# Seven-product down projection for all eight pairs of tiles, with h of tiles 0–3 normalised on GpSimd

## The chip, the cores and the metric

The kernel runs on one core of a Trainium2 chip. The metric is device time in microseconds (us) of one execution. The profile covers one execution; its span is about 2 us shorter than the measured time. PE is TensorE, PEld its weight load, DVE is VectorE, ACT is ScalarE, POOL is GpSimd, SP issues the DMA. "L244" is line 244 of the kernel that is being profiled; the change moves most lines by a few, so the table of lines below gives both numbers. In the profile lines `arena` is the kernel's on-chip buffer, `ps` the eight accumulator banks that TensorE writes, and `x8` a count.

## The reference, cut to what matters

```
xn = layernorm(x)                                  # x is 2048 x 512
# A: linear attention, 32 heads of 16, q, k, v = xn @ wqkv
phi = concat(softmax(p), softmax(-p))              # for q and k, p = q @ w_phi or k @ w_phi
kv  = sum over tokens of phi_k^T v;  z = sum of phi_k
A   = (phi_q kv / phi_q z) @ wo
# B: bilinear gated unit, F = 1792
h   = (xn @ w_gate) * (xn @ w_up)
out = x + A + h @ w_down
```

Layernorm of a token is a subtraction of the mean and a factor `rstd`. Everything in B is linear in that factor twice, so h of a token that was not normalised is right up to a factor r2 = rstd². The kernel uses this for its first four tiles (of 128 tokens), in order to start the matmuls before the statistics are there.

## The kernel before

A list scheduler inside the kernel decides in which order each engine gets its instructions; each engine then runs its own list strictly in order and waits on semaphores. TensorE alternates between 56 gate units (8 matmuls of 512 columns; ScalarE copies the gate half, VectorE multiplies it with the up half) and the features of queries and keys.

The features hand work round the engines: TensorE makes p, ScalarE takes two exponentials, VectorE sums, ScalarE inverts, and GpSimd scales the second softmax. The query buffers are a ring of three (`RQ = 3`).

```python
def features(name, t, w, b=None):                  # w = 0: query, 1: key
    s = t % (RK if w else RQ)
    ...                                            # (cut: matmul, two exps on ACT)
    dve(lambda e: e.tensor_reduce(out=sm, in_=e_v, axis=AX.X, op=ALU.add), ...)         # L511
    ...                                            # (cut: 1/sum on ACT)
    pool(lambda e: e.tensor_tensor(out=rat, in0=sm[:, :, 0], in1=rs[:, :, 1], op=ALU.mult), ...)   # L519
    pool(lambda e: e.tensor_tensor(out=e_v[:, :, 1, :], in0=e_v[:, :, 1, :], ...)       # L521
```

The down projection has two forms. Tiles 0–3 use `out_tile`, 18 matmuls of 512 columns each, because r2 can then be applied at the eviction. Tiles 4–15 use `out_pair`: two tiles of h and w_down are cut into 2 x 2 blocks, and seven products replace eight (7 x 7 matmuls, and 16 for the attention heads: 65 of 256 columns). It needs sums and differences of the blocks, in half precision, made by VectorE (`h_combine`, `wd_combine`). These mix two tiles, so r2 must be in h before them.

```python
def out_tile(t, between):                          # tiles 0-3
    mm(ps, [(hT_v[:, ft, tok], wdh_v[:, ft, :]) for ft in range(NF)], ..., stop=False)  # 14 x 512 columns
    between()
    mm(ps, [(oT_tile(t)[:, q, :], wo_v[:, q, :]) for q in range(NQ)], ..., start=False) # 4 x 512 columns
    dve(lambda e: e.scalar_tensor_tensor(out=stg, in0=ps, scalar=ri[:, t:t + 1], in1=xr_tile(t), ...)

def d_scale():                                     # powers of two that keep h and w_down in fp16's range
    power_of_two(swd, ...)
    pool(lambda e: e.tensor_tensor(out=scl[:, 22:23], in0=sh, in1=swd, op=ALU.mult), ["sh", "swd"], ["both"], 1)
    dve(lambda e: e.reciprocal(out=scl[:, 23:24], in_=scl[:, 22:23]), ["both"], ["rboth"], 1)
```

The last two lines matter later: a product of two single numbers sits in GpSimd's list, and VectorE's list holds an instruction that waits for it.

The softmax here doesn't subtract the row's maximum and nothing guards it: scores larger than these inputs give would overflow.

Of the kernel before, what the change touches and what calls it, by code (L numbers as in the profile page):

```python
# [24 lines left out]
ND = 4  # L25
# [28 lines left out]
class _Sched:  # L54
# [10 lines left out]
    def _record(self, st, reads, writes, free=()):  # L65
        deps = {}

        def need(d, raw):
            if d is None or d is st:
                return  # L70
            if d.lane == st.lane and (st.eng == PE or not raw):
                return
            deps[id(d)] = d

        for k in reads:
            assert k in self.writer, f"{k} is read unwritten"
            need(self.writer.get(k), True)
            self.readers.setdefault(k, []).append(st)
        for k in writes:
            w = self.writer.get(k)  # L80
            assert w is None or w is st or self.readers.get(k) or k in reads or st.lane == w.lane or k in free, f"{k} is overwritten unread"
            need(w, False)
            for r in self.readers.get(k, ()):
                need(r, False)
            self.writer[k] = st
            self.readers[k] = []
        st.deps = list(deps.values())
# [36 lines left out]
def _build(nc, es, A_x, A_wqkv, A_w_phi, A_wo, B_w_gate, B_w_up, B_w_down, out):  # L124
# [210 lines left out]
    load_gu(SP, 3)  # L335
    sc.pin = False
# [230 lines left out]
    epsz = sbf("epsz", 0, 1)  # L567
    kvz_v = sb("kvz", 0, 8 * CW).rearrange("p (c j) -> p c j", c=8)

    def kv_finish():  # L570
        sc.prio = 0
        for hb in range(2):
            dve(lambda e, hb=hb: e.tensor_tensor(
                out=kvz_v[:, hb * 4:hb * 4 + 4, :], in0=bank(hb, 0, 4 * CW).rearrange("p (c j) -> p c j", c=4),
                in1=mask[:, None, :].to_broadcast([128, 4, CW]), op=ALU.mult),
                [("ps", hb), "mask"], [("kvz", hb, 0)], 4 * CW)
            z = bank(hb, 0, 4 * CW).rearrange("p (c h j) -> p c h j", c=4, h=4)[:, :, :, 16]
            mz = mask.rearrange("p (h j) -> p h j", h=4)[:, None, :, 16].to_broadcast([128, 4, 4])
            oz = kvz_v[:, hb * 4:hb * 4 + 4, :].rearrange("p c (h j) -> p c h j", h=4)[:, :, :, 16]
            dve(lambda e, z=z, mz=mz, oz=oz: e.scalar_tensor_tensor(out=oz, in0=z, scalar=epsz, in1=mz, op0=ALU.add,  # L580
                                                                    op1=ALU.mult),
                [("ps", hb), "mask", "epsz", ("kvz", hb, 0)], [("kvz", hb)], 16)
        sc.prio = 1
# [25 lines left out]
    def num_stage(t):  # L609
        ph = ph_tile(t)  # L610
        b0 = 2 * (t % 2) if t < ND else 0
# [13 lines left out]
        k, key = upscale(t)  # L625
        act(den_v[:, r], nd[:, :, :, 16], ps, [("den", r)], func=ACTF.Ln)
        act(w_v[:, r], den_v[:, r], [("den", r), key], [("w", r)], func=ACTF.Exp, scale=-1.0, bias=k)
# [15 lines left out]
    ri, lnup = scl[:, 4:4 + ND], scl[:, 26:26 + ND + 1]  # L643

    def upscale(t):
        return (lnup[:, t + 1:t + 2] if t < ND else lnup[:, 0:1]), "lnup"

# [3 lines left out]
    def squares(src, i, after):  # L651
        j = NF - 8 + squared[0] % 8
        squared[0] += 1
        junk = hT_v[:, j, 3 * 512:4 * 512]
        if src == "wd":
            i_ap, key, col, o_ap = wd_v[:, i, :], ["wd"], 28 + i, junk
        else:
            v, col = (wg_v, i) if src == "wg" else (wu_v, 14 + i)
            i_ap, o_ap = v[:, :, i * 128:(i + 1) * 128], junk.rearrange("p (a b) -> p a b", a=NQ)
            key = [(src, max(k for k, (lo, _) in enumerate(SLICES) if lo <= i * 128))]  # L660
        act(o_ap, i_ap, key + after + ([("junk", j)] if squared[0] > 8 else []), [("junk", j), ("ssq", col)],
            func=ACTF.Square, accum=ssq[:, col:col + 1])
# [20 lines left out]
    def h_scale():  # L683
        norms(0, 28, 2)
        pool(lambda e: e.tensor_tensor(out=scl[:, 20:21], in0=scl[:, 12:13], in1=scl[:, 13:14], op=ALU.mult),
             [("rn", 0)], ["rgu"], 1)
        power_of_two(sh, scl[:, 20:21], ["rgu"], "sh", 8.0)


    def d_scale():  # L690
        norms(28, 14, 1)
        power_of_two(swd, scl[:, 18:19], [("rn", 28)], "swd", 4096.0)
# [3 lines left out]
        dve(lambda e: e.reciprocal(out=scl[:, 24:25], in_=swd), ["swd"], ["rswd"], 1)  # L696
        power_of_two(scl[:, 25:26], scl[:, 24:25], ["rswd"], "iswd", 1.0009765625)
        pool(lambda e: e.tensor_scalar(out=ri, in0=r2, scalar1=scl[:, 25:26], scalar2=None, op0=ALU.mult),
             ["iswd", "r2"], ["ri"], 4)
        act(lnup[:, 1:1 + ND], ri, ["ri"], ["lnri"], func=ACTF.Ln, scale=1.0)  # L700
        act(scl[:, 23:25], scl[:, 0:2], ["sh", "swd", "inv", "iswd"], ["lns"], func=ACTF.Ln)
        pool(lambda e: e.tensor_scalar(out=lnup[:, 1:1 + ND], in0=lnup[:, 1:1 + ND], scalar1=-1.0, scalar2=None,
                                       op0=ALU.mult), ["lnri"], ["lnup4"], 4)
        pool(lambda e: e.tensor_tensor(out=lnup[:, 0:1], in0=scl[:, 23:24], in1=scl[:, 24:25], op=ALU.add),
             ["lns", "lnup4"], ["lnup"], 1)
# [7 lines left out]
    def to_half(sg):  # L713
        sc.prio = 2
        for i in range(7):
            sl = slice(2 * i, 2 * i + 2)
            ks = [("hT", ft, sg) for ft in (2 * i, 2 * i + 1)]
            dve(lambda e, sl=sl: e.tensor_scalar(out=hH_v[:, sl, sg * 512:(sg + 1) * 512],  # L718
                                                  in0=hT_v[:, sl, sg * 512:(sg + 1) * 512], scalar1=sh, scalar2=None,
                                                  op0=ALU.mult), ks + ["sh"], ks, 1024, 0.35)  # L720
        sc.prio = 1


# [5 lines left out]
    def wd_combine(k):  # L729
# [6 lines left out]
        sc.prio = 2  # L736
# [5 lines left out]

    def h_block(t, i):
        return hH_v[:, i * NK:(i + 1) * NK, t * 128:(t + 1) * 128]

    def s_block(p, k):
        return h_block(2 * p + 1, 0) if k == 3 else sw_v[:, p % RS, {1: 0, 2: 1, 4: 2}[k]]

    def s_key(p, k):
        return ("s3", p) if k == 3 else ("s", p % RS, k)  # L750

    def h_combine(p):
        t0, t1 = 2 * p, 2 * p + 1
        a11, a12, a21, a22 = (h_block(t, i) for t in (t0, t1) for i in range(2))
        ks = [("hT", ft, t0 // 4) for ft in range(NF)] + ["ups"]
        sc.prio = 2
        for k, i0, i1, op, more in ((1, a21, a22, ALU.add, []),
# [4 lines left out]
                ks + more, [s_key(p, k)], NK * 128, 0.55)  # L762
        sc.prio = 1

    glu = [0]

# [23 lines left out]
    def gate(ft, sg, bg, bu, s):  # L790
        g = sb("g", s * 512, 512)
        if sg < 3:
            act(g, bank(bg), [("ps", bg)], [("g", s)])
        else:
            act(g, bank(bg), [("ps", bg), "sh"], [("g", s)], func=ACTF.Identity, scale=sh)
        sc.prio = 0
        h_v = hT_v if sg < 3 else hH_v
        dve(lambda e: e.tensor_tensor(out=h_v[:, ft, sg * 512:(sg + 1) * 512], in0=bank(bu), in1=g, op=ALU.mult),  # L798
            [("ps", bu), ("g", s)] + ([("junk", ft)] if sg == 3 and ft >= NF - 8 else []), [("hT", ft, sg)], 512)
        sc.prio = 1  # L800

    def out_tile(t, between):
        b = 4 + t % 2
        sg = t // 4
        tok = slice(t * 128, (t + 1) * 128)
        ps = bank(b)
        mm(ps, [(hT_v[:, ft, tok], wdh_v[:, ft, :]) for ft in range(NF)],
           [("hT", ft, sg) for ft in range(NF)] + [("wdh", i) for i in range(7)], b, stop=False)
        between()
        mm(ps, [(oT_tile(t)[:, q, :], wo_v[:, q, :]) for q in range(NQ)], [("phT", t), "wo"], b, start=False)  # L810
        stg = sb("ostg", (t % 3) * 512, 512)
        dve(lambda e: e.scalar_tensor_tensor(out=stg, in0=ps, scalar=ri[:, t:t + 1], in1=xr_tile(t), op0=ALU.mult,
                                             op1=ALU.add), [("ps", b), ("xr", t % 4), "ri"],
            [("ostg", t % 3, 0), ("ostg", t % 3, 1)], 512)
        store(t, 0, 512, [0, 1])
# [30 lines left out]
    def out_pair(p, fill):  # L846
# [4 lines left out]
        first = [("g", i) for i in range(4)] if p == ND // 2 else []  # L851
# [25 lines left out]
        product(BC, s_block(p, 4), b22, hk + [s_key(p, 4)])  # L877
# [79 lines left out]
    def late_loads(t):  # L957
        sc.pin = True
        if t == 0:
            load_x(8, 4)  # L960
        elif t == 1:
# [8 lines left out]
    def scales(t):  # L970
        last = [("hT", *latest[0])] if latest[0] else []
        if 3 <= t < 10:
            for i in range(2 * (t - 3), 2 * (t - 2)):
                squares("wg", i, last)
                squares("wu", i, last)
        elif t == 11:
            h_scale()
        if 10 <= t < 15:
            for i in range(14 * (t - 10) // 5, 14 * (t - 9) // 5):
                squares("wd", i, last)  # L980
        if t == 13:
            to_half(1)
        elif t == 16:
            d_scale()
            to_half(2)
        elif t == 17:
            wd_combine(1)
            wd_combine(2)
            wd_combine(3)

# [15 lines left out]
    for t in range(NT + 3):  # L1006
# [11 lines left out]
        scales(t)  # L1018
# [6 lines left out]
        if t >= 12:  # L1025
            q_next()
        if t < 2:
            v_scale(t, t)
        else:
            up()  # L1030
            if t >= 10:
# [3 lines left out]
            if t < NT + 1:  # L1035
# [3 lines left out]
    assert not waiting  # L1039
    wd_combine(4)  # L1040
    num_stage(0)
    for t in range(0, 4, 2):
        load_residual(t)
    up(len(ups))
    for p in range(ND // 2, ND // 2 + RS):
        h_combine(p)
    num_stage(1)
    for t in range(ND):
        out_tile(t, lambda: num_stage(t + 2))
        if t % 2:  # L1050
            load_residual(t + 3)
    for p in range(ND // 2, NT // 2):
        plan = [[], [2 * p + 2], [2 * p + 3]]

        def fill():
            for t in plan.pop(0):
                if t < NT:
                    num_stage(t)
        out_pair(p, fill)
        if p + 2 < NT // 2:  # L1060
            load_residual(2 * p + 4)
        if p + RS < NT // 2:
# [148 lines left out]
```

## Time and profile before

The median of the first three runs was 219.1 us (218.66 to 219.12).

| what | line before | line after | mean, before | mean, after |
|---|---|---|---|---|
| matmuls of 512 / 256 columns, PE | L244 | L244 | 215.6 / 109.1 ns | the same |
| sum of features, DVE | L511 | L512 | 1.21 us | 1.21 us |
| gate multiplication, DVE | L798 | L817 | 0.68 us | 0.68 us |
| v scaling, DVE | L549 | L550 | 0.68 us | 0.68 us |
| w_down in half precision, 1024 columns, DVE | L709 | L699 | 0.59 us | 0.88 us |
| `wd_combine`, 1792 columns, DVE | L737 | L748 | 1.21 us | 1.50 us |
| `h_combine`, 896 columns, DVE | L761 | L778 | 0.62 us | 0.72 us |
| ratio and its multiplication, POOL | L519, L521 | L520, L522 | 0.27, 1.09 us | 0.29, 1.08 us |
| product of the two scales, POOL | L693 | L693 | 0.20 us | 0.20 us |
| normalisation of h, POOL | | L727 | | 1.26 us |

From the page of the kernel before: span, busy time (share of the span, number of instructions), and the chain of waits, that is the work that ended last followed back to what released each piece.

```profile
span 216.7 us, 3958 instructions
PE 211.9 (98%) x1434; PEld 121.0 (56%) x1434; DVE 159.6 (74%) x275; ACT 134.0 (62%) x366; POOL 63.4 (29%) x135
PE 95%; DVE 2%; DMA 1%; ACT 0%; issue 0%; DVEq 0%
```

TensorE is the limit, and 95% of the chain is its own work. Whatever shortens its stream shortens the kernel; any other engine costs time only when TensorE waits for it.

The chain in order of time, kernel before; columns are start, duration, what. First around 27 us, then the end of `out_tile` and a pair of seven products.

```profile
27.08 1.20 DVE arena L511
28.29 0.61 DVE arena L798
...
28.94 3.19 PE ps L244 x14
...
155.29 0.26 PE ps L617 x8
155.54 3.88 PE ps L244 x18
...
163.57 0.26 PE ps L617 x8
...
175.23 4.69 PE ps L244 x43
...
182.84 2.18 PE ps L244 x20
```

Two tiles of `out_tile` with two numerator stages (L617, the features of the queries times kv) take 163.57 − 155.29 = 8.28 us, a pair with the same two stages 182.84 − 175.23 = 7.61 us. At 27 us the chain leaves TensorE: it waits for a gate multiplication (L798) that stands behind a sum (L511) on VectorE. VectorE's timeline, kernel before, says why that was late (the bracket is the idle time before the instruction and what ended it).

```profile
26.47 0.69 DVE L400 BATCH_NORM_STATS2 arena<-arena 128x6 f32<-128x512 bf16 x1 [1.89 <-DMA arena<-in_A_x_dram]
27.08 1.20 DVE L511 TENSOR_REDUCE arena<-arena 128x64 f32<-128x1024 bf16 x1
28.20 1.27 DVE L798 TENSOR_TENSOR arena<-ps,arena 128x512 bf16<-128x512 f32 x2
```

VectorE stood for 1.89 us in front of the statistics of tile 8, whose x was loaded late.

Busy time by stretch, kernel before: stretch and its length, then PE, PEld, DVE, ACT, POOL (each with its count), PE clock, DMA share, GB/s.

```profile
100.00:110.00 10.00, 10.00 (x55) 4.70 (x54) 9.79 (x15) 9.34 (x28) 5.70 (x9) 1.00 0.28 55
110.00:120.00 10.00, 10.00 (x59) 4.70 (x57) 7.88 (x12) 8.76 (x25) 4.83 (x9) 1.00 0.33 65
120.00:130.00 10.00, 10.00 (x62) 4.78 (x59) 7.71 (x9) 7.40 (x19) 4.04 (x7) 1.00 0.44 55
```

TensorE is full here; VectorE is 77 to 98% busy and GpSimd 40 to 57%.

### The profile page before, as it was taken

The numbers are of one execution on the slowest core, as the hardware profiler recorded it, in microseconds if no ns is written. First come the engines' busy times: TensorE is split into PE (matmuls) and PEld (weight loads), VectorE is DVE, ScalarE is ACT, GpSimd is POOL, SyncE is SP. The second block draws the span as 40 slices with busy tenths as digits, with TensorE's granted clock in tenths as the row PEclk, the third lists the DMA queues.
The fourth block names the chain that finished last, engine by engine and source line by source line (L and its number), as shares of the span: only waits on it lengthen the run. The fifth ranks groups of instructions, "written<-read, shape, count | busy, mean of one in ns | idle before, by whom it ended". The sixth has DMA issues, their size and how long they took to land.

```text
span 216.7 us, 3958 instructions
## 1 busy us (share of the span) xinstructions
PE 211.9 (98%) x1434; PEld 121.0 (56%) x1434; DVE 159.6 (74%) x275; ACT 134.0 (62%) x366; POOL 63.4 (29%) x135
## 2 busy tenths in 40 slices
PE   7999989999999999999999999999999999999994
PEld 2564434444444454444444444454445889999983
DVE  3858699998656545779997767999999486565332
ACT  5568848978977787697898865666400433333330
POOL 3032633431222032316447255334310201220220
DMA  5998991179400000012042263264655346433351
GB/s 185 294 310 280 196 172 25 27 237 279 94 0 0 0 0 5 13 35 48 19 82 48 48 76 72 48 122 124 123 121 143 88 86 101 122 98 98 111 86 48
DMA packets 48403, 22.03 MB, mean 102 GB/s; under 512 B 37504, under 2 KB 46848, under 8 KB 48384
## 3 DMA queue, kind: packets, MB, share of 16 engines
q1 hardware_dynamic: 47440, 21.13, 43.4%
q10 hardware_dynamic: 944, 0.66, 1.0%
q8 instruction: 11, 0.18, 0.4%
q14 instruction: 8, 0.07, 0.1%
HBM read 10.76 MB, written 2.10 MB: 59 GB/s over the span
## 4 chain that ended last, share of the span: by engine, by line
PE 95%; DVE 2%; DMA 1%; ACT 0%; issue 0%; DVEq 0%
PE ps L244 90%; PE ps L617 2%; PE ps L561 2%; DMA arena<-in_A_x_dram 1%; PE ps L373 1%; PE ps L479 1%; DVE arena L511 1%; DVE arena L422 0%; DVE arena L798 0%; ACT arena L225 0%; DVE arena L838 0%; DVE arena L429 0%; DVE arena L354 0%; PE ps L901 0%; DVE arena L355 0%
## 5 line engine op out<-in xcount | busy, mean ns | idle before, releaser
L244 PE MATMUL ps<-arena 128*128 128x512 bf16 (+3 forms) x1118 | 203.3, 339 | 0.9 <-DVE arena L798 0.9
L244 PEld LDWEIGHTS ps<-arena 128*128 128x128 bf16 (+1 forms) x1118 | 106.6, 98 | 81.3 <-DVE arena L798 1.4
L225 ACT ACTIVATE arena<-ps 128x512 bf16<-128x512 f32 (+4 forms) x118 | 58.9, 535 | 43.2 <-PE ps L617 26.8
L225 ACT ACTIVATE arena<-arena 128x32 f32<-128x32 f32 (+6 forms) x147 | 52.4, 365 | 13.7 <-DVE arena L511 10.3
L798 DVE TENSOR_TENSOR arena<-ps,arena 128x512 bf16<-128x512 f32 (+1 forms) x56 | 37.8, 683 | 16.2 <-ACT arena L225 12.7
L511 DVE TENSOR_REDUCE arena<-arena 128x64 f32<-128x1024 bf16 x32 | 38.8, 1215 | 10.7 <-ACT arena L225 10.6
L521 POOL TENSOR_TENSOR arena<-arena 128x512 bf16<-128x512 bf16 x32 | 34.7, 1085 | 1.2
L519 POOL TENSOR_TENSOR arena<-arena 128x32 f32<-128x32 f32 x32 | 8.6, 268 | 72.7 <-ACT arena L225 42.1
L225 ACT ACTIVATE arena<-ps,arena 128x512 bf16<-128x512 f32 (+1 forms) x36 | 22.7, 651 | 7.4 <-PE ps L244 7.2
L838 DVE SCALAR_TENSOR_TENSOR arena<-ps,arena 128x256 bf16<-128x256 f32 x24 | 11.3, 483 | 17.6 <-PE ps L244 17.6
L858 POOL TENSOR_TENSOR arena<-arena 128x256 f32<-128x256 f32 x12 | 7.8, 670 | 44.4 <-ACT arena L225 44.4
L225 ACT ACTIVATE ps<-ps 128x256 f32<-128x256 f32 x18 | 6.6, 368 | 12.5 <-PE ps L244 12.5
L761 DVE TENSOR_TENSOR arena<-arena 128x896 f16<-128x896 f16 x24 | 14.0, 616 | 0.0
L628 DVE TENSOR_TENSOR arena<-ps,arena 128x512 bf16<-128x512 f32 x16 | 11.0, 689 | 3.6 <-ACT arena L225 3.4
L400 DVE BATCH_NORM_STATS2 arena<-arena 128x6 f32<-128x512 bf16 x16 | 10.5, 671 | 2.3 <-DMA arena<-in_A_x_dram 2.3
L549 DVE TENSOR_TENSOR arena<-ps,arena 128x512 bf16<-128x512 f32 x14 | 9.6, 683 | 0.1
L225 ACT ACTIVATION_READ_ACCUMULATOR arena<-arena 128x1 f32 x46 | 8.7, 188 | 0.0
L458 POOL TENSOR_SCALAR arena<-arena 128x1 f32<-128x1 f32 x12 | 3.2, 284 | 17.0 <-ACT arena L225 17.0
L561 PEld LDWEIGHTS ps<-arena 128*128 128x128 bf16 x128 | 6.1, 97 | 3.5
L718 DVE TENSOR_SCALAR arena<-arena 128x1024 f16<-128x1024 bf16 x14 | 7.6, 603 | 0.0
L617 PEld LDWEIGHTS ps<-arena 128*128 128x128 bf16 x128 | 6.1, 97 | 1.8 <-ACT arena L225 0.4
L617 PE MATMUL ps<-arena 128*128 128x68 bf16 x128 | 6.7, 194 | 0.0
(53 smaller groups left out, 65.4 us busy)
## 6 DMA issues: line engine op xcount, KB each, us to landing
arena<-in_A_x_dram SPq DMA_DIRECT2D x9, 256.0 KB, 3.0
out_dram<-arena SPq DMA_DIRECT2D x15, 128.0 KB, 2.0
arena<-in_B_w_down_dram SPq DMA_DIRECT2D x1, 1792.0 KB, 7.8
arena<-in_A_x_dram SPq DMA_DIRECT2D x3, 512.0 KB, 4.6
arena<-arena SPq DMA_TRANSPOSE x44, 3.0
arena<-in_B_w_gate_dram SPq DMA_DIRECT2D x1, 640.0 KB, 8.8
arena<-in_B_w_up_dram SPq DMA_DIRECT2D x1, 640.0 KB, 10.0
arena<-in_B_w_gate_dram SPq DMA_DIRECT2D x1, 512.0 KB, 5.0
```

Of the source, the lines that this page charges most:

```text
L225: return sc.step(ACT, lambda e: e.activation(out=out_ap, in_=in_ap, func=func, scale=scale, **kw), reads, writes, 130.0 + 0.833 * n)
L244: ins = e.matmul(out_ap, lhsT=l, rhs=r, start=start and i == 0, stop=stop and i == npair - 1, **kw)
L400: dve(lambda e: e.bn_stats(stats_v[:, t, 0:6], x_tile(t)), [("x", t)], [("st", t)], 512)
L511: dve(lambda e: e.tensor_reduce(out=sm, in_=e_v, axis=AX.X, op=ALU.add), [(name, s, 0), (name, s, 1)], [("sums", sr)], 1024)
L521: pool(lambda e: e.tensor_tensor(out=e_v[:, :, 1, :], in0=e_v[:, :, 1, :], in1=rat[:, :, None].to_broadcast([128, H, 16]), op=ALU.mult), [ ...
L549: dve(lambda e: e.tensor_tensor(out=vs_tile(t)[:, :, 0:16], in0=src.rearrange("p (h f) -> p h f", h=H), in1=rp.unsqueeze(2).to_broadcast([ ...
L561: ins = e.matmul(bank(c // 4, (c % 4) * CW, CW), lhsT=ek[:, c * 128:(c + 1) * 128], rhs=vs[:, c * CW:(c + 1) * CW], start=(t == 0 and c % ...
L617: ins = e.matmul(bank(b0 + c // 4, (c % 4) * CW, CW), lhsT=ph[:, c, :], rhs=kvz_v[:, c, :], start=True, stop=True)
L628: dve(lambda e: e.tensor_tensor(out=o_tile(t).rearrange("p (b h f) -> p b h f", b=2, f=16), in0=nd[:, :, :, 0:16], in1=w_v[:, r].unsqueeze ...
L761: dve(lambda e, k=k, i0=i0, i1=i1, op=op: e.tensor_tensor(out=s_block(p, k), in0=i0, in1=i1, op=op), ks + more, [s_key(p, k)], NK * 128, 0.55)
L798: dve(lambda e: e.tensor_tensor(out=h_v[:, ft, sg * 512:(sg + 1) * 512], in0=bank(bu), in1=g, op=ALU.mult), [("ps", bu), ("g", s)] + ([("j ...
L838: dve(lambda e: e.scalar_tensor_tensor(out=stg, in0=bank(b, 0, 256), scalar=inv, in1=resid, op0=ALU.mult, op1=ALU.add), [("ps", b), rkey, ...
```

## The change

The intent: all eight pairs go through seven products. r2 becomes a row (128 partitions all hold the 512 tokens' factors), by way of DRAM: a small write, then a broadcast read. GpSimd multiplies h of tiles 0–3 with it in 14 instructions. The power-of-two scale of the heads, which was a bias in an exponential of each tile's numerator stage, goes into the kv matrix. x of tiles 8–11 is loaded before the loop. ScalarE's squares of the gate and up weights become half as many, of twice the size, and w_down's go to VectorE. Four of the 16 query features move from the gate stage into pairs 1–4. The call of `d_scale`, with its product of two numbers on GpSimd, moves from token tile 16 to 12. The full diff also moves half conversions and combinations and adds a dependency between ScalarE's own uses of an accumulator bank. The core of it, with cuts:

```diff
     load_gu(SP, 3)
+    load_x(8, 4)                                   # and no longer in the loop at t == 0
...
+    def row_of_r2():
+        pool(lambda e: e.tensor_scalar(out=r2s, in0=r2, scalar1=sh, ...), ["r2", "sh"], ["r2s"], 4)
+        row = nc.dram_tensor("r2row", (ND, 128), F32, kind="Internal").ap()
+        o = row.rearrange("t p -> p t")
+        sc.dma(SP, lambda e: e.dma_start(o, r2s, allow_slow_non_contiguous=True), ["r2s"], ["r2row"], 131072)
+        ks = [("x", 14), ("x", 15)]
+        wide = bass.AP(tensor=row.tensor, offset=row.offset, ap=[[0, 128], [1, ND * 128]])
+        sc.dma(SP, lambda e: e.dma_start(r2w, wide), ["r2row"], ["r2w"] + ks, 262144, free=ks)
+
+    def normalise(fts):
+        sc.prio = 2
+        for ft in fts:
+            pool(lambda e, ft=ft: e.tensor_tensor(out=hH_v[:, ft, 0:512], in0=hT_v[:, ft, 0:512], in1=r2w,
+                                                  op=ALU.mult), [("hT", ft, 0), "r2w", ("x", 14), ("x", 15)],
+                 [("hT", ft, 0)], 512)
...
 def wd_combine(k):
-        sc.prio = 2
+        sc.prio = 1
...
 def scales(t):
+        if t == 11:
+            row_of_r2()
+        elif t == 12:
+            d_scale()
...
+        if 13 <= t < 17:
+            normalise(range(14 * (t - 13) // 4, 14 * (t - 12) // 4))
...
-    for t in range(ND):
-        out_tile(t, lambda: num_stage(t + 2))
-    for p in range(ND // 2, NT // 2):
+    for p in range(NT // 2):
         ...
         out_pair(p, fill)
```

## The prediction

> **What bounds it.** TensorE. On the page PE is busy 98%; the chain of waits is 95% PE. Read from that chain, 18 matmuls of 512 columns take 3.88 us (215.6 ns each), 43 of 256 columns 4.69 us (109.1 ns). The Trainium skill ("TensorE: Matmul & The Clock Gate", section "Wait — 56ns, not 53.3ns?") gives N/2.4 GHz plus about 2.5 ns for a warm array; the trace agrees, so there is no slack inside the stream. TensorE waits only at the start (4.7 us), once at 28.0 us (0.90 us idle, timeline), for 0.4 us before the first numerator stage, and in the tail after its last matmul (about 3 us).
>
> **What the change removes.** (1) Tiles 0-3 today take two chains of 18 matmuls per pair, 8.28 us with two numerator stages (155.29 to 163.57). A seven-product pair takes 65 matmuls of 256 columns, 7.61 us (175.23 to 182.84). Two pairs: 2 x 0.67 = 1.34 us, all on TensorE. (2) The load of x tiles 8-11 moves ahead of the first transpose in the DMA queue. Before, it was issued at 21.87 us, behind a transpose that waited for VectorE; VectorE sat 1.89 us idle for it until 26.47, then still had to do a 1.2 us reduction ahead of the gate multiply that TensorE was waiting for at 28.0. I expect that 0.90 us to go.
>
> **What moves, off the chain.** ScalarE: 28 + 14 squares (0.62 + 0.19 us each, 34 us) become 14 of twice the size (estimate 1.2 us each). VectorE: seven squares of 1,024 columns, about 1.2 us each, at 64-93 us, where it is 48-63% busy; 14 half conversions (0.60 us) become nine, all after the gate stage; eight combinations (0.62 us) more; four 1.2 us reductions move into pairs 1-4. GpSimd: 14 multiplications, about 1.1 us each (as its 128x512 multiply, 1.085), 15.4 us within 100-145 us, where it is 40-57% busy; roughly 90% after. It stays inside, with three tiles of slack before the kv products need its result. The row by DRAM costs TensorE nothing.
>
> **New waits?** VectorE after the last gate, my hand count: half conversion of tiles 4-7 and the combinations for pair 1 are done about 11 us into the pair stage, the operands of pair 2 at about 15-16 us; TensorE wants them at 16.1. So little margin, no large wait. The skill ("GPSIMD Engine Reference", section "1. Specifications") says that GpSimd shares its SBUF interface with VectorE instructions with two SBUF inputs; this trace agrees: the 1,792-column subtraction took 1.58 us beside a GpSimd multiply, 1.08 without. I allow 0.3 us for waits from this and from the first numerator stage, which now has two gate units (3.45 us) instead of three behind kv.
>
> **Prediction.** 219.1 - 1.34 - 0.90 + 0.3 = 217.2 us. Eight in ten: 216.3 to 218.9. Faster by over 2%: 0.03; within 2%: 0.94; slower by over 2%: 0.03.
>
> **What would show each step.** (1) In the chain, pairs of tiles 0-3 at 7.6 us, no 512-column output chains; PE busy down by about 1.3 us. (2) The idle piece at 26-29 us gone from the chain, and VectorE's statistics of tile 8 no longer waiting for x. (3) GpSimd busy about 79 us, near 90% between 105 and 145 us; ScalarE some 17 us less busy. (4) TensorE gapless from 30 us to the last matmul; any gap would be at the start of pairs 1-3 (waiting for VectorE) or before the first numerator stage.
>
> **What would make it wrong.** GpSimd or its shared interface slows VectorE enough that gates come late at 110-145 us, or the first pair waits for the normalised h; the in-order VectorE queue runs behind in pairs 1-4; the early x load delays weights and the 28 us gap stays or moves.

## More of the kernel before

The kernel before ran again beside every experiment; its medians are between 218.73 and 219.22. The experiments ran on five chips, so each is compared with the kernel before in its own rounds.

Between consecutive starts of matmuls this wait is worth 1.06 us over the normal spacing.

## The result, and the profile after

The changed kernel took 220.94 us (median of 4 runs, 220.86 to 221.3), the kernel before 219.11 in the same rounds: ratio 1.009, 95% interval 1.0072 to 1.0109. It is correct. It is within 2%, but reliably slower, where 217.2 was predicted.

The page of the kernel after:

```profile
span 219.1 us, 4039 instructions
PE 211.5 (97%) x1472; PEld 127.2 (58%) x1492; DVE 176.9 (81%) x293; ACT 126.2 (58%) x316; POOL 84.4 (39%) x151
PE 78%; DVE 6%; issue 5%; POOL 5%; DMA 3%; ACT 1%; SPq 0%; POOLq 0%
```

The chain is only 78% PE now; GpSimd and VectorE, which had next to nothing of it, have 11%. Pairs of tiles 0–3 in the chain of the kernel after:

```profile
156.15 0.26 PE ps L619 x8
...
158.80 0.26 PE ps L619 x8
...
164.62 0.26 PE ps L619 x8
```

The expected saving is there: from the numerator stage of one pair to that of the next is 164.62 − 156.15 = 8.47 us, and this now includes four matmuls of 512 columns for a query (4 x 215.6 ns = 0.86 us) that used to be in the gate stage; without them it is 7.61 us. The wait at 27 us is gone too: TensorE's timeline shows one unbroken piece from 23.73 us for 8.58 us. TensorE's timeline, kernel after, shows where it was lost.

```profile
111.16 3.52 PE L244 MATMUL ps<-arena 128*128 128x512 bf16 x8 [1.98 <-DVE arena L665]
```

TensorE is idle for 1.98 us (2.14 us over the normal spacing of starts). Then eight matmuls take 3.52 us: the record of the clock that TensorE was granted is at 0.5 (half speed) for 3.413 us from 111.3 us on, which stretches the work in it by about 1.7 us. The releaser named, L665, is a tiny instruction. By the data it is the gate multiplication just before it, L817, which ended at 110.42 + 0.68 = 111.10. VectorE's timeline, kernel after:

```profile
109.23 0.16 DVE L694 RECIPROCAL arena<-arena 128x1 f32<-128x1 f32 x1 [3.94 <-POOL arena L693]
109.31 1.20 DVE L512 TENSOR_REDUCE arena<-arena 128x64 f32<-128x1024 bf16 x1
110.42 0.68 DVE L817 TENSOR_TENSOR arena<-ps,arena 128x512 f16<-128x512 f32 x1
111.02 0.14 DVE L665 TENSOR_SCALAR arena<-arena 128x1 f32<-128x1 f32 x1
```

VectorE stood 3.94 us in front of the reciprocal of the product of the two scales, and with it everything behind it in its list: a sum and the gate multiplication. The product (L693) is one number, 0.20 us on GpSimd. GpSimd's timeline, kernel after:

```profile
91.33 1.06 POOL L522 TENSOR_TENSOR arena<-arena 128x512 bf16<-128x512 bf16 x1
99.12 2.28 POOL L727 TENSOR_TENSOR arena<-arena 128x512 f16<-128x512 bf16 x2 [6.73 <-DMA arena<-r2row]
...
105.42 3.40 POOL L727 TENSOR_TENSOR arena<-arena 128x512 f16<-128x512 bf16 x3
...
109.00 0.20 POOL L693 TENSOR_TENSOR arena<-arena 128x1 f32<-128x1 f32 x1
```

GpSimd stood 6.73 us in front of the first normalisation, waiting for the row, and then had the ratios that had become ready meanwhile and the normalisations to do, without a pause. The product of the scales came at its turn. The DMA issues of this stretch, kernel after (size, us from issue to landing), show how long the row took:

```profile
arena<-r2row SPq DMA_DIRECT2D x1, 256.0 KB, 4.6
r2row<-arena SPq DMA_DIRECT2D x1, 2.0 KB, 8.1
```

Two KB took 8.1 us to write (as 512 pieces of 4 bytes), the broadcast 4.6 us. The Trainium skill ("DMA: Bandwidth & Descriptors", section "Specifications") says that transfers need 512 bytes and more for line rate and that smaller ones cost a read-modify-write; the trace agrees in direction (2 KB took longer than 256 KB), while no run here shows the read-modify-write itself. Busy by stretch, kernel after, same columns as before:

```profile
100.00:110.00 10.00, 9.13 (x49) 4.08 (x48) 5.25 (x8) 5.08 (x14) 9.92 (x14) 1.00 0.14 28
110.00:120.00 10.00, 8.79 (x39) 3.84 (x41) 10.00 (x16) 6.25 (x16) 9.84 (x14) 0.83 0.30 59
120.00:130.00 10.00, 9.84 (x52) 4.48 (x52) 9.97 (x11) 6.51 (x16) 8.76 (x10) 1.00 0.25 49
```

GpSimd went from 4.0–5.7 to 8.8–9.9 us in ten. First VectorE and ScalarE idle behind it (100 to 110 us: 5.25 and 5.08), then VectorE is full.

The sum closes, on the start of the last matmul in the profiled executions. Before it was 213.68 us. Less 1.34 (pairs) and 1.06 (wait at 27 us) it would be 211.28. To this the kernel after adds 2.14 us at 109–111 us, about 1.7 of half clock and 0.27 at 126 us, in all 4.1 us, and 0.8 of longer waits for the first weights at 5–7 us. That last wait varies by itself: it was between 0.1 and 1.4 us over all kernels run here, whatever their edit. That makes 216.2; measured is 216.18.

### The profile page after: what moved, and what is told of

Its sections match the earlier page's. It is cut to its first block, busy times and chain, and to the rows that moved or that the text cites. A ratio compares the mean times of both kernels' runs of the same rounds, so it can differ in the third digit from the quotient of the medians. Undisturbed runs are those within 1.5% of the kernel's fastest.

```text
span 219.1 us, 4039 instructions
## 1 busy us (share of the span) xinstructions
PE 211.5 (97%) x1472; PEld 127.2 (58%) x1492; DVE 176.9 (81%) x293; ACT 126.2 (58%) x316; POOL 84.4 (39%) x151
## 4 chain that ended last, share of the span: by engine, by line
PE 78%; DVE 6%; issue 5%; POOL 5%; DMA 3%; ACT 1%; SPq 0%; POOLq 0%
PE ps L244 74%; POOL arena L727 3%; DMA arena<-in_A_wqkv_dram 3%; DVE arena L512 3%; PE ps L619 2%; DVE arena L699 2%; DVE arena L817 1%; PE ps L562 1%; POOL arena L522 1%; ACT arena L225 1%; PE ps L374 1%; POOL arena L520 1%; DVE arena L550 0%; SPq L269 0%; DVE arena L842 0%
## 5 line engine op out<-in xcount | busy, mean ns | idle before, releaser
L244 PE MATMUL ps<-arena 128*128 128x512 bf16 (+2 forms) x1156 | 201.6, 330 | 3.8 <-DVE arena L665 2.0
L244 PEld LDWEIGHTS ps<-arena 128*128 128x128 bf16 (+1 forms) x1176 | 112.4, 98 | 78.8 <-DVE arena L665 2.5
L225 ACT ACTIVATE arena<-ps 128x512 bf16<-128x512 f32 (+4 forms) x107 | 53.3, 530 | 37.6 <-PE ps L619 16.5
L225 ACT ACTIVATE arena<-arena 128x32 f32<-128x32 f32 (+7 forms) x117 | 38.8, 345 | 21.3 <-DVE arena L512 18.1
L817 DVE TENSOR_TENSOR arena<-ps,arena 128x512 bf16<-128x512 f32 (+1 forms) x56 | 38.0, 683 | 8.2 <-ACT arena L225 4.5
L225 ACT ACTIVATE arena<-ps,arena 128x512 bf16<-128x512 f32 (+1 forms) x49 | 31.0, 653 | 12.2 <-PE ps L244 12.1
L778 DVE TENSOR_TENSOR arena<-arena 128x896 f16<-128x896 f16 x32 | 22.1, 715 | 0.0
L727 POOL TENSOR_TENSOR arena<-arena 128x512 f16<-128x512 bf16 x14 | 17.4, 1255 | 6.7 <-DMA arena<-r2row 6.7
L654 DVE SCALAR_TENSOR_TENSOR arena<-arena 128x1024 bf16<-128x1024 bf16 x7 | 11.9, 1721 | 0.0
L550 DVE TENSOR_TENSOR arena<-ps,arena 128x512 bf16<-128x512 f32 x14 | 9.5, 682 | 0.0
L562 PEld LDWEIGHTS ps<-arena 128*128 128x128 bf16 x128 | 6.2, 99 | 3.9 <-issue 0.6
L562 PE MATMUL ps<-arena 128*128 128x68 bf16 x128 | 6.6, 195 | 0.0
L619 PE MATMUL ps<-arena 128*128 128x68 bf16 x128 | 6.5, 194 | 0.0
```

The source lines that it names most:

```text
L225: return sc.step(ACT, lambda e: e.activation(out=out_ap, in_=in_ap, func=func, scale=scale, **kw), reads, writes, 130.0 + 0.833 * n)
L244: ins = e.matmul(out_ap, lhsT=l, rhs=r, start=start and i == 0, stop=stop and i == npair - 1, **kw)
L562: ins = e.matmul(bank(c // 4, (c % 4) * CW, CW), lhsT=ek[:, c * 128:(c + 1) * 128], rhs=vs[:, c * CW:(c + 1) * CW], start=(t == 0 and c % ...
L654: dve(lambda e: e.scalar_tensor_tensor(out=junk, in0=i_ap, scalar=1.0, in1=i_ap, op0=ALU.mult, op1=ALU.mult, accum_out=ssq[:, col:col + 1] ...
L727: pool(lambda e, ft=ft: e.tensor_tensor(out=hH_v[:, ft, 0:512], in0=hT_v[:, ft, 0:512], in1=r2w, op=ALU.mult), [("hT", ft, 0), "r2w", ("x" ...
L778: dve(lambda e, k=k, i0=i0, i1=i1, op=op: e.tensor_tensor(out=s_block(p, k), in0=i0, in1=i1, op=op), ks + more, [s_key(p, k)] + over.get(k ...
```

## The experiments

The theory: GpSimd falls behind, because its list stops for the row and because the normalisations fill it, and it passes the delay on by the product of the scales in its list. Rivals: (a) the half clock is the loss and the wait only its trigger; (b) the sharing of memory access between GpSimd and VectorE slows VectorE; (c) VectorE has simply too much work; (d) the gains themselves are not what the trace says. Each edit is against the kernel after, but where it says otherwise. Read each time against the expectation above it: those of e1, e2, e3 and e9 to e15 missed it, several because a second wait came up where the first was taken away. "Gap" below is the excess over the normal spacing between the starts of two matmuls.

### The product of the scales on VectorE (e1)

```diff
-        pool(lambda e: e.tensor_tensor(out=scl[:, 22:23], in0=sh, in1=swd, op=ALU.mult), ["sh", "swd"], ["both"], 1)
+        dve(lambda e: e.tensor_tensor(out=scl[:, 22:23], in0=sh, in1=swd, op=ALU.mult), ["sh", "swd"], ["both"], 1)
```

> The changed kernel with one instruction moved: the product of the two scales (one element per partition) is done on VectorE instead of GpSimd. Theory Q (queue): in the changed kernel VectorE stood still 3.94 us at 105-109 us, in order behind a reciprocal that waited for this product, and the product stood in GpSimd's queue behind multiplications of h that had started late, after 6.73 us of waiting for the row from DRAM. TensorE then idled 1.98 us and ran 3.41 us at half clock (1.71 us lost). Q expects both gone: 220.9 - 1.98 - 1.71 = about 217.3 us, clock 1.000, no wait of VectorE for that product. Theory C (contention: VectorE is simply slowed by GpSimd's 17 us of multiplications on the shared interface, its 896-column operations took 715 ns instead of 616) expects little change, 220 us or more.

Measured: 219.33 us, before 218.87, ratio 1.0024 (1.0005 to 1.0043). VectorE's wait for L693 and the half clock are gone, but a gap of 1.78 us stands at 112.7 us, and smaller ones (0.33, 0.17, 0.48) follow. From this run's timeline of all engines:

```profile
98.85 2.29 POOL L727 TENSOR_TENSOR arena<-arena 128x512 f16<-128x512 bf16 x2 [7.13 <-DMA arena<-r2row]
...
113.44 0.60 ACT L225 ACTIVATE arena<-ps 128x512 bf16<-128x512 f32 x1 [4.09 <-PE ps L244]
...
114.70 1.47 PE L244 MATMUL ps<-arena 128*128 128x512 bf16 x6 [1.61 <-ACT arena L225]
```

Now ScalarE is what stands, 4.09 us. The releaser named is not the one; the chain of the same run has it:

```profile
108.86 1.13 POOL arena L522
...
110.04 3.04 DMA arena<-arena
...
113.44 1.21 ACT arena L225 x3
```

The exponential of a query waits for its buffer in the ring of three, that is for the transposing DMA that reads the old query. This was issued at 110.04 us, when GpSimd's ratio multiplication of 108.86 us was done, and took 3.04 us. GpSimd had done three normalisations before it, from 104.97 us on. So the product was one path by which GpSimd's delay came out; under it lay another, at nearly the same time. Against the kernel before of its rounds the run is 0.5 us slower, where the kernel after was 1.8.

### Work for TensorE in the gap, to keep the clock up (e2)

```diff
+        if i == 40:                                 # gate unit that waited: 9 dummy matmuls of 512 columns before it
+            def dummy(e): ...
+            sc.step(PE, dummy, [], [("ps", bg)], 9 * 216.0)
```

> The changed kernel with nine 512-column matmuls of ones put on TensorE just before the spot where it idled 1.98 us (into a bank that is free there and is overwritten by the real product). They fill the wait and do not shorten it. Theory Q with the clock as a consequence of the idle time: the half clock of 3.41 us goes, the 1.98 us stay: 220.9 - 1.7 = about 219.2 us, clock 1.000. If the half clock came from something else than the idle TensorE, the clock record stays at 0.992 and the time at 220.9 us or more.

Measured: 222.81 us, ratio 1.0182 (1.0145 to 1.0218). The clock stayed at 1.0 and the filler took 1.94 us, in the place of the wait. Yet waits of 0.54, 1.67 and 1.89 us came at 111, 116 and 122 us. So keeping the clock up did not shorten the kernel: other waits came in the place of the half clock. That GpSimd catches up while TensorE runs slowly is my reading and not shown; at 122 us TensorE waits for a VectorE that is full. The repeats of the kernel after agree: one of its four runs had a clock of 1.0 instead of 0.992, and took 221.01 us, no less than the others (it was not traced). Rival (a) falls as the whole of the loss: at full clock 2.8 us of gaps stand in e1 and 4.1 here, beside the filler. What the half clock costs by itself is not shown.

### The normalisations left out (e6)

```diff
-        if 13 <= t < 17:
-            normalise(range(14 * (t - 13) // 4, 14 * (t - 12) // 4))
+        if t == 13:
+            normalise(range(1))                     # wrong result on purpose: 1 of 14
```

> The changed kernel with 13 of the 14 multiplications of h on GpSimd left out (the result of tiles 0-3 is wrong on purpose); the row's trip, the query tiles in the pair stage and the product of the scales on GpSimd stay. Theory Q (as the first runs sharpened it: GpSimd, held 6.7 us by the row and then fully busy from 99 to 124 us, delivers late; TensorE pays either through VectorE's wait for the product of the scales or through ScalarE's wait for a free one of three query buffers): no wait of TensorE between 100 and 145 us, clock 1.000, 217.0 us (216.5 to 217.6). If VectorE's or ScalarE's own load were the cause, waits of 1 us or more stay there, 218.5 us or more.

Measured: 216.54 us, before 218.85, ratio 0.9895 (0.987 to 0.9919); the result is wrong (relative error 0.155). After 7.3 us no gap is left but one of 0.19 us. TensorE's timeline, and the group of the one normalisation left (busy time, mean ns, idle time before it):

```profile
110.89 8.79 PE L244 MATMUL ps<-arena 128*128 128x512 bf16 x40
...
L727 POOL TENSOR_TENSOR arena<-arena 128x512 f16<-128x512 bf16 x1 | 1.2, 1167 | 7.2 <-DMA arena<-r2row 7.2
```

GpSimd still waited 7.2 us for the row, and the product of the scales was still in its list. So the wait for the row alone costs nothing, and (c) falls as well: VectorE has nearly the same work here (busy 174.8 us against 176.9). Of its means, `wd_combine` fell from 1.50 to 1.29 us and w_down's conversion from 0.88 to 0.66, but `h_combine` stayed at 0.71: its 0.72 does not come from the normalisations. The loss is the 13 multiplications on GpSimd, or what they do to others.

### The row fetched early (e3, e10, e11)

```diff
+        elif t == 4:                                # 6 in the second version: after the load of w_down
+            row_out()                               # write r2 (not yet scaled) to DRAM
+        elif t == 7:                                # 10 in the second
+            row_in()                                # fetch it; GpSimd multiplies the row by sh later
```

> The changed kernel with the row of 1/var sent to DRAM and fetched long before it is needed (into a tile that is unused then), and the head scale multiplied onto the row by GpSimd afterwards; the product of the scales stays on GpSimd. Theory Q: GpSimd no longer waits 6.73 us for the row, its multiplications start some 10 us earlier, the product of the scales comes before VectorE needs it: about 217.3 us (216.8 to 218), clock 1.000. If the row's trip through DRAM is not the cause, the wait of VectorE stays and the time is 220 us or more.

> As e3_row_early, but with the row's write and its fetch at spots of the DMA queue where no large load follows (e3 lost 5 us at 59 us to the 1.8 MB load behind the row's 9.7 us write); the product of the scales stays on GpSimd. Theory Q: no wait of GpSimd for the row; its multiplications start at about 88 us; the product of the scales is due before VectorE asks for it or under 1 us late; TensorE waits under 1 us in 100-145 us, clock 1.000: about 217.6 us (217.0 to 218.5).

The third has the edit of the second, and the product on VectorE:

> e10 with the product of the scales on VectorE as well: both ways by which GpSimd's lateness reached TensorE are closed. Theory Q: 217.2 us (216.8 to 217.8), faster than the kernel before by about 0.8%. If VectorE slowed by the shared interface is a cause of its own, waits of TensorE of 0.5 us or more in 100-145 us stay.

Measured: 226.18 (ratio 1.0333), 227.01 (1.0379) and 227.08 us (1.0387). All three missed, for a reason of their own: a wait of TensorE at 58–66 us, idle for 5.08, 7.14 and 7.19 us, with 7 to 10 us of half clock that begins within it. DMA issues of the second at 44 to 75 us:

```profile
arena<-in_B_w_down_dram SPq DMA_DIRECT2D x1, 1792.0 KB, 7.9
...
arena<-arena SPq DMA_TRANSPOSE x7, 9.5
r2row<-arena SPq DMA_DIRECT2D x1, 2.0 KB, 13.2
```

The transposes of x took 9.5 us in the median, where the median of all 44 in the kernel before is 3.0: they were issued behind the small write, and that behind the big loads. (In the first the order was the other way: the 1,792 KB load of w_down stood behind the small write, and took 15.4 us instead of 7.8.) The rest of these runs suggests that the wait at 109 us went down (a gap of 0.8 us at 122–124 us is the largest later one in the first two, one of 1.16 us at 136 us in the third), but with TensorE 7 us later everything else has more time, so they decide nothing about it.

### The normalisations later (e9)

```diff
-        if 13 <= t < 17:
-            normalise(range(14 * (t - 13) // 4, 14 * (t - 12) // 4))
+        if 14 <= t < 18:
+            normalise(range(14 * (t - 14) // 4, 14 * (t - 13) // 4))
```

The product is on VectorE here as well.

> The changed kernel with the product of the scales on VectorE (as in e1) and the multiplications of h queued one token tile later, so that GpSimd is not in front of one while the row is on its way. Theory Q: GpSimd's wait for the row falls from 7.1 us to under 2 us, ScalarE's 4.1 us wait for a query buffer goes, TensorE's 1.8 us wait at 113 us goes: about 217.5 us (217.0 to 218.2), against 219.3 in e1. If it is the load alone (17.4 us of multiplications next to three query/key tiles per token tile) and not the wait for the row, a wait of 1.5 us or more comes back some 9 us later, and the time stays at 219 us.

Measured: 219.58 us, ratio 1.0039 (1.0017 to 1.0061), with a gap of 1.82 us at 113.5. The edit did not do what it was for. The scheduler goes by its own estimate of when the row lands; it put the first normalisations behind the last ratio again, and GpSimd waited 7.2 us as before. To place an instruction one needs a dependency.

### Each normalisation behind the latest h (e12)

```diff
-  [("hT", ft, 0), "r2w", ("x", 14), ("x", 15)],
+  [("hT", ft, 0), "r2w", ("x", 14), ("x", 15), ("hT", *latest[0])],
```

With the product on VectorE. The new dependency is on a gate product that is made at the time wanted, so the multiplications spread out.

> e9 did not do what it was meant to: the list order still put the first two multiplications right behind the last ratio, and GpSimd waited 7.2 us for the row as before. Here each multiplication also waits for the latest h of its token tile (a true dependency, so the order has to change), the product of the scales on VectorE as in e1. Theory Q: GpSimd's wait for the row is gone, it serves the ratios on time until about 103 us and multiplies in its gaps; ScalarE's 4 us wait for a query buffer goes; TensorE waits under 0.5 us in 100-145 us: 217.3 us (216.8 to 218.0). Theory L (load alone: 17.4 us of multiplications do not fit beside the ratios, whenever they start): waits of 1.5 us or more in 110-150 us, 219 us.

Measured: 218.24 us, before 219.22, ratio 0.9947 (0.9915 to 0.9978). The wait for the row is gone, and ScalarE's four microseconds, and the gap at 109–113 us. One gap is left, 1.45 us at 127.4: there TensorE waits for the v scaling (L550), which frees an accumulator bank. From this run's timeline of all engines:

```profile
117.79 2.06 DVE L699 TENSOR_SCALAR arena<-arena 128x1024 f16<-128x1024 bf16 x2
...
118.23 5.74 POOL L727 TENSOR_TENSOR arena<-arena 128x512 f16<-128x512 bf16 x4
...
119.89 1.93 DVE L748 TENSOR_TENSOR arena<-arena 128x1792 f16<-128x1792 f16 x1
...
123.47 1.44 DVE L748 TENSOR_TENSOR arena<-arena 128x1792 f16<-128x1792 f16 x1
...
128.29 0.68 DVE L550 TENSOR_TENSOR arena<-ps,arena 128x512 bf16<-128x512 f32 x1
```

VectorE is full, and its half-precision instructions beside GpSimd's four multiplications are long.

### The row written in pieces of 16 bytes (e13, e14)

```diff
-        row = nc.dram_tensor("r2row", (ND, 128), F32, kind="Internal").ap()
-        o = row.rearrange("t p -> p t")
+        row = nc.dram_tensor("r2row", (128, ND), F32, kind="Internal").ap()
+        o = row                                     # and GpSimd reads the row with a stride of 4
```

> e1 with one thing changed: the row is written to DRAM as 128 runs of 16 bytes instead of 512 of 4 bytes (the multiplication reads it with a stride). The write took 8.1 us to land in the changed kernel. Expected: 2.5 to 4 us, GpSimd's wait for the row 7.1 us to about 2.5 us. Theory Q: TensorE's 1.8 us wait at 113 us goes or falls under 0.5 us, about 217.8 us. Theory L: it stays, 219.3 us.

> e12 and e13 together. If e12 already takes away every wait for the row, the same time as e12 within 0.3 us; the 16-byte row then only frees the DMA queue for the first query transposes.

Measured, with the product on VectorE: 218.81 us, ratio 0.9971 (0.9939 to 1.0003). The write took 1.4 us instead of 8.1, GpSimd no longer waited for the row, and the gap at 109–113 us is gone. So the late row was needed for that gap as much as the multiplications were. The strided row made a multiplication longer, 1.51 us, and two gaps (0.55 and 1.45 us) stand at 126–128. With the dependency on h as well (the second text) it was worse, 221.26 us (220.32 to 223.03), ratio 1.0112 (1.006 to 1.0163): the multiplications took 1.58 us, and four gaps of 0.24 to 1.45 us lie between 124 and 152 us.

### Four multiplications left out (e18)

The kernel of the dependency on h, without the four multiplications that ran at 118–124 us; the result is wrong (relative error 0.087). The order of TensorE and VectorE is the same.

```diff
         for ft in fts:
+            if 3 <= ft < 7:
+                continue
```

> e12 without the four multiplications of h that run at 118-124 us (wrong result for tiles 0-3 on purpose); VectorE's and TensorE's order are those of e12. If the shared interface is the cause of the 1.45 us wait at 127 us: the 1,792-column subtractions there take 1.1 us each instead of 1.93 and 1.44, the conversions before them 0.5 us, and the wait falls under 0.3 us: about 217.0 us. If VectorE's order and load are the cause, the wait stays above 1 us and the time at 218.2 us.

Measured: 216.41 us, before 219.0, ratio 0.9886 (0.9854 to 0.9918). The gap at 127 us is gone. VectorE's timeline, to be held against the lines above (L748 there is L750 here):

```profile
117.52 1.15 DVE L699 TENSOR_SCALAR arena<-arena 128x1024 f16<-128x1024 bf16 x2
118.71 1.09 DVE L750 TENSOR_TENSOR arena<-arena 128x1792 f16<-128x1792 f16 x1
...
121.44 1.08 DVE L750 TENSOR_TENSOR arena<-arena 128x1792 f16<-128x1792 f16 x1
```

The same instructions took 1.15 instead of 2.06 (a pair), 1.09 instead of 1.93 and 1.08 instead of 1.44 us. The Trainium skill ("GPSIMD Engine Reference", section "1. Specifications") says that GpSimd shares its SBUF interfaces with VectorE and names the VectorE instructions that contend; this agrees, and here it is 0.91 + 0.84 + 0.36 = 2.11 us on VectorE, enough for the gap of 1.45 us. So (b) holds, but for this second wait only, and there together with VectorE's order, which alone can also take the gap away (next section). The sharing is no part of the first one: VectorE stood idle then, and GpSimd's five multiplications at 105–109 and 99–101 us took 3.40 / 3 = 1.13 and 2.28 / 2 = 1.14 us each, no longer than the 1.17 us of the only one in e6 (times on GpSimd are rough).

### Other orders on VectorE (e15, e16)

Two more, on the kernel with the dependency on h: the v scaling at the highest priority, or `wd_combine` back at its old low one.

```diff
+        sc.prio = 0                                 # around the v scaling (first version)
...
-        sc.prio = 1                                 # in wd_combine (second version)
+        sc.prio = 2
```

> e12 with the scaling of v (which frees the accumulator bank that the next query product needs) put before VectorE's other ready work. The multiplications and their contention stay. If the order is what makes the wait: gone or under 0.5 us, about 217.0 us, the fastest correct kernel so far. If contention leaves VectorE with too much work whatever its order, a wait of 1 us or more comes back elsewhere, 218 us.

> e12 with the subtractions of w_down's blocks back at the low priority that they had in the kernel before (the change raised it): they move behind the reductions and the scaling of v. If the raised priority made the wait at 127 us: under 0.5 us there, about 217.1 us. Otherwise 218.2 us.

Measured: 218.04 us, ratio 0.9961 (0.9933 to 0.9989), and 217.6 us, 0.9957 (0.9909 to 1.0004, one run at 219.26). In both the gap at 127 us is gone. In the place of it one of 1.26 or 0.85 us stands at 149: VectorE waited 1.99 or 1.18 us for the last multiplication of GpSimd before the first `h_combine`, which pushed the last gate multiplications, and with them the first pair, back.

### Only the early load of x, in the kernel before (e5, twice)

```diff
     load_gu(SP, 3)
+    load_x(8, 4)
...
-        if t == 0:
-            load_x(8, 4)
-        elif t == 1:
+        if t == 1:
```

This one is against the kernel before. It ran twice, the second time with more rounds.

> The kernel before with only one part of the change: the load of x tiles 8-11 is issued before the loop. By the prediction TensorE's 0.90 us wait at 28 us goes: about 218.2 us against 219.1. If the wait only moves (to another operand or to the start), the time stays at 219.1.

> The same kernel as e5 with more rounds: its trace had lost TensorE's wait at 28 us (1.06 us between two matmul starts beyond the usual spacing), its time was only 0.1 us lower with an interval of -0.3% to +0.25%. Expected by the trace: 0.4 to 0.9 us below the kernel before. If the early load costs elsewhere what it saves, 0 to 0.3 us.

Measured: 218.73 us, ratio 0.9996 (0.9968 to 1.0025), and 218.33 us, ratio 0.9953 (0.9928 to 0.9978). In both traces the gap at 27.7 us is absent. The time of the first batch shows nothing, that of the second (6 runs) 0.9 us less. Together with the trace I take the gain of about 1 us as real; the waits for the first weights, which vary as much, hide it in four runs.

### All remedies together (e19)

The product on VectorE, the dependency on h, `wd_combine` at its old priority, and the multiplications one token tile earlier, so that the last is done before `h_combine` wants it:

```diff
-        if 13 <= t < 17:
-            normalise(range(14 * (t - 13) // 4, 14 * (t - 12) // 4))
+        if 12 <= t < 16:
+            normalise(range(14 * (t - 12) // 4, 14 * (t - 11) // 4))
```

> e16 with the multiplications of h queued one token tile earlier (each still waits for the latest h of its tile, the first ones at about 99 us, when the row lands). If the wait at 148.6 us is lateness of the last multiplication: VectorE's 1.2 us wait for GpSimd before the first combination goes, TensorE waits under 0.3 us between 10 us and its last matmul: 217.0 us (216.6 to 217.6), about 0.9% faster than the kernel before. If the load only shifts, a wait of 1 us or more shows at 110-130 us and the time is 217.6 us or more.

Measured: 216.47 us (216.01 to 216.69), before 218.73, ratio 0.9899 (0.9882 to 0.9915). It is correct, and the fastest correct kernel. Its page (busy and chain):

```profile
PE 210.2 (98%) x1492; PEld 126.6 (59%) x1492; DVE 178.3 (83%) x294; ACT 126.2 (59%) x316; POOL 85.9 (40%) x150
PE 96%; DMA 1%; DVE 1%; issue 0%
```

And the first normalisation in GpSimd's timeline of the same kernel:

```profile
99.35 3.40 POOL L727 TENSOR_TENSOR arena<-arena 128x512 f16<-128x512 bf16 x3 [1.23 <-DMA arena<-r2row]
```

No gap over 0.19 us is left after 6 us. The last matmul starts at 211.33 us, where the sum above asked for 211.28: both gains in full. (The expectation was 217.0 us; the time is a little below its range.) GpSimd does the same work as in the kernel after (85.9 us against 84.4); it waits for the row 1.23 us instead of 6.73, because the ratios that are ready in the meantime now stand in front of it. VectorE is busier than in the kernel after (178.3 us), and no gap comes of it. So (d) falls too, and (c) a second time.

## Why the prediction was right or wrong

The prediction was 217.2 us with a range up to 218.9; measured were 220.94. It gave 0.94 to "within 2%", which is where the result lies, but it expected it on the other side of the kernel before.

- **Minus 1.34 us for two pairs: right.** A pair of tiles 0–3 takes 7.61 us without the query that moved there, and the last matmul of the final version is where this term puts it.
- **Minus 0.90 us at 28 us: right,** shown by the trace of the kernel after, and by those of the early load alone, of whose two batches of times one shows it. By starts of matmuls it was 1.06 us.
- **ScalarE: right in the squares,** whose two groups fell from 26.5 + 8.7 to 14.6 + 0.6 + 3.4 us, 16.6 where 17 was said. But all its busy time fell by only 7.8 us (134.0 to 126.2), where the prediction's third sign was some 17; it is not the limit.
- **The squares of w_down on VectorE: mis-sized,** 1.72 us each, not 1.2. They lie at a time at which no wait of TensorE came of it.
- **VectorE in pairs 1–3: right,** that "little margin, no large wait" held: the only gap over 0.15 us behind 130 us is 0.19, at the first pair.
- **Plus 0.3 us for new waits: this is where it failed,** measured 4.1 us, the half clock included. The step that failed is "It stays inside, with three tiles of slack before the kv products need its result. The row by DRAM costs TensorE nothing." The first half counted GpSimd's work against its busy share (it came to 31.24 of 40 us, 78%, at 105–145 us, less than the 90% said, though the multiplications took 17.4 us and not 15.4) and against the last consumer of the result. The slack that counts is that of every other instruction in the same list. The row was counted as a transfer off the path; but its 8.1 + 4.6 us hold up an in-order list for 6.73 us, which costs nothing alone (e6) and a good part of the loss together with the multiplications.

What took its place, as the runs showed: GpSimd stops for the row, then has normalisations of 1.26 us between the ratios. Take away either the multiplications (e6) or the wait for the row (e12, e13), and the gap at 109–113 us is gone. The delay came out first by a one-number product, which the change had moved into this stretch and of which the prediction says nothing, and, that moved, by the ring of three query buffers. The prediction named "GpSimd or its shared interface slows VectorE enough that gates come late at 110-145 us" as what would make it wrong. The time and the victim are right. The means in the kernel after was a semaphore, not the interface; the interface is the means of the wait at 127 us, which is seen only once the first is mended. The half clock behind the gap was not foreseen; e1 and the filler show that a loss is left without it.

What stays open: why the kernel after lost its clock in three of its four runs and not in the fourth, what the half clock costs by itself, and how much of the 0.27 us gap at 126 us is the interface.

## What to carry to other kernels

Before moving work to a half-idle engine with an in-order list, look at what else stands in that list: the smallest instruction behind a late input delays whoever reads it, and a ring of buffers passes it on, so check every consumer and not the busy share. When one such path is cut and the time hardly moves, look for the next at the same place: leaving out the suspected work, even with a wrong result, tells what all such paths together are worth. An instruction that waits for a DMA belongs behind the ready work, by a real dependency if the scheduler's estimate of the DMA is wrong.

## What the Trainium skill lacked or had wrong

- "TensorE: Matmul & The Clock Gate", section "What's actually happening": it gives half clock after at least one idle window of about 3.4 us. Here 1.98 us of idle TensorE were followed by a record of 3.413 us at 0.5, the length of the page's window; one of four runs of the same kernel kept its clock, and 1.61 us (e1) and 1.72 us (e2) had no such record. In e3, e10 and e11 the record begins 2.6 to 3.8 us into a wait. So shorter waits than the section's rule can cost the clock, in some runs. (The page's spacing of matmuls, N/2.4 GHz plus about 2.5 ns, section "Wait — 56ns, not 53.3ns?", is confirmed: 215.6 and 109.1 ns.)
- "GPSIMD Engine Reference", section "1. Specifications": it names the sharing with VectorE but no size ("SBUF — State Buffer" has the rule of who blocks whom, but no times for such a pair). Here a 1,792-column fp16 subtraction on VectorE took 1.08 us without them and up to 1.93 beside GpSimd multiplications, a pair of 1,024-column scalings 1.15 and 2.06; GpSimd's multiplication took 1.17 us when it was the only one and 1.26 in the mean of the kernel after.
- "DMA: Bandwidth & Descriptors", section "Specifications": it gives a limit of 512 bytes but no time for far smaller pieces, nor for how it goes with their number. Here 2 KB took 8.1 us as 512 pieces of 4 bytes and 1.4 us as 128 pieces of 16 bytes. In the run with the write right behind large loads it took 13.2 us, and transposes issued behind it 9.5 us in the median.
